# Clamp and shift of the float64 weight decode as scalar_tensor_tensor with a constant in PSUM, in place of tensor_scalar

## The chip, the cores and the metric

The kernel runs on one core of one Trainium2 chip. The metric is the device time of one execution in microseconds (us).

## What is computed

A two-dimensional Fourier transform (real part), then two dense networks over its 6016 tokens of 256 features. All weights arrive as float64, and the kernel turns them into float32 on the chip.

```python
X = np.fft.fft(np.fft.fft(x, axis=1), axis=2).real      # x: (2, 3008, 256)
x = X.reshape(6016, 256)
gate = 1.0 / (1.0 + np.exp(-(x @ w_gate)))              # first network, d_ff 1536
x = gate * (x @ w_val) @ moe_w_out
h = x @ w_in                                            # second network, d_ff 2048
out = (h * np.cos(h)) @ moe2_w_out
```

## The kernel before, in words

Three stages follow one another: the transform (stages a, b and c, to about 83 us of the profile), the first network (to about 518 us) and the second network (to the end). The transform leaves the tokens in `eo[t]`, six tiles of 2 x 1004 columns, each an even and an odd half. Every float32 operand of a matmul is split into a high and a low part, so that one product takes three matmuls (`three`, L493 to L495).

The first network runs 72 **steps**, `step1(s)`, s = 12 t + f, for six token tiles t and twelve blocks f of 128 hidden features. TensorE (PE) does 24 matmuls of 128x502 in a step:

- `ab(s, 0)` (6 matmuls) into PSUM banks 4 and 5, then `ab(s, 1)` (6 matmuls) into banks 6 and 7. The last three of `ab(s, 1)` write bank 7.
- `out1(s - 4)` (12 matmuls, L533, L535, L536) into banks 0 to 3; the four L533 stand at its end.

VectorE (DVE) then serves `even(s)`, two L511 that read banks 4 and 5, and `tokens(s)`, two L519 that read banks 6 and 7. These four banks have no second copy: `ab(s + 1, 0)` waits for the L511 of step s, `ab(s + 1, 1)` for its L519. ScalarE (ACT) takes the sigmoid (L667), GpSimd (POOL) multiplies gate and value (two L523, `times`), ACT makes the high part (L607, L608), and a DMA from POOL's queue (L546) adds the low part.

Beside this, 35 **units** of weights are decoded, each 128x512 float64 (the first smaller). A unit is a list of steps in `dec_steps` and `unit_steps`: a load (SP's queue, L148), two activations on ACT (L123, L124), then on VectorE the clamp (L127), the left shift by three (L129) and the sign (L131), on POOL an integer add (L134), and the split into high and low part (L139 on ACT, L140 mostly on POOL). Units of the second network are written to DRAM (`ws`, L167) and loaded again into `wr` late in the first network (L551). The tokens of the next tile are split into `es` in the same way (L139, L140) at the steps 5 and 6 of the first tile and around the steps 17, 29, 41, 53 and 64.

What runs between the fixed instructions is set by a planner at build time: `fill(e, until)` puts a unit's next step on engine e as long as its estimated cost (the number in the step's tuple, plus `beside[0]` = 0.5 us for VectorE in the first network) ends before `until`. So a change of a cost moves instructions, on VectorE and, through the times when units become ready, on the other engines' queues.

The clamp and the shift before are

```python
(V, .34, lambda: V.tensor_scalar(out=every(t), in0=every(t), scalar1=FMIN, scalar2=FMAX,
                                 op0=ALU.max, op1=ALU.min)),
(V, .34, lambda: V.tensor_scalar(out=every(u), in0=every(u), scalar1=3, scalar2=0x7FFFFFFF,
                                 op0=ALU.logical_shift_left, op1=ALU.bitwise_and)),
```

where t is the unit's 128x512 float32 buffer in SBUF, u the same bytes as uint32, and `every` a view of 2 x 256.

Of the kernel before, what the change touches and what calls it, by code (L numbers as in the profile page):

```python
# [12 lines left out]
U32 = mybir.dt.uint32  # L13
AF = mybir.ActivationFunctionType
ALU = mybir.AluOpType
# [29 lines left out]
FMIN = float(np.uint32(0x38000000).view(np.float32)) * 2.0 ** -80  # L45
FMAX = float(np.uint32(0x47EFFFFF).view(np.float32)) * 2.0 ** -80
# [3 lines left out]
def fft_moe_moe(ctx: ExitStack, tc: tile.TileContext, x, x0, head, w1, w1s, wo1, w2, t1, t3, out):  # L50
# [10 lines left out]
    V, A, G, PE = nc.vector, nc.scalar, nc.gpsimd, nc.tensor  # L61
# [8 lines left out]
    ps = pp.tile([128, 8, 512], F32, name="ps")  # L70
# [33 lines left out]
    VG = (V, G)  # L104

    def spend(e, us, after=0.0):
        clk[e] = max(clk[e], after) + us
        return clk[e]

    def dec_steps(buf, n):  # L110

        r = buf[:, 0:2 * n].rearrange("p (n t) -> p n t", t=2)
        lo, hi = r[:, :, 0], r[:, :, 1]
        t = buf[:, 2 * n:3 * n]
        u = t.bitcast(U32)

        def every(a):

            return a.rearrange("p (n k) -> p k n", k=2)

        return [

            (A, .52, lambda: A.activation(out=t, in_=hi, func=AF.Abs, scale=2.0 ** -80)),  # L123
            (A, .52, lambda: A.activation(out=lo.bitcast(I32), in_=lo.bitcast(U32), func=AF.Copy,  # L124
                                          scale=2.0 ** -29)),

            (V, .34, lambda: V.tensor_scalar(out=every(t), in0=every(t), scalar1=FMIN, scalar2=FMAX,  # L127
                                             op0=ALU.max, op1=ALU.min)),
            (V, .34, lambda: V.tensor_scalar(out=every(u), in0=every(u), scalar1=3, scalar2=0x7FFFFFFF,  # L129
                                             op0=ALU.logical_shift_left, op1=ALU.bitwise_and)),  # L130
            (V, .6, lambda: V.scalar_tensor_tensor(out=u, in0=hi.bitcast(U32), scalar=0x80000000, in1=u,  # L131
                                                   op0=ALU.bitwise_and, op1=ALU.bitwise_or)),

            (G, 1.23, lambda: G.tensor_tensor(out=t.bitcast(I32), in0=t.bitcast(I32), in1=lo.bitcast(I32),  # L134
                                              op=ALU.add)),
        ]
# [7 lines left out]
    def unit_steps(kind, i, buf):  # L144
        n = 2 * NF1 if kind == "row" else UC
        src = {"row": w1s, "w1": w1[i % NF1], "wo1": wo1[i % 6], "w2": w2[i]}[kind]
        t = buf[:, 2 * n:3 * n]
        steps = [(DQ, 1.5 * n / UC, lambda: DQ.dma_start(out=buf[:, 0:2 * n].bitcast(U32), in_=src.bitcast(U32)))]  # L148
        steps += dec_steps(buf, n)
        if kind == "row":  # L150
            steps.append((A, .2, lambda: A.copy(w128, t)))
        elif kind == "w1":

            d, m = t[:, 0:256], t[:, 256:512]
            steps += [(VG, .34, lambda e: e.tensor_tensor(out=buf[:, 0:256], in0=d, in1=m, op=ALU.add)),
                      (VG, .34, lambda e: e.tensor_tensor(out=buf[:, 256:512], in0=d, in1=m, op=ALU.subtract))]
            steps += hilo_steps(W1[:, i, :, :, 0], W1[:, i, :, :, 1],
                                buf[:, 0:512].rearrange("p (e g m) -> p g e m", e=2, g=2))
        elif kind == "wo1":
            steps += hilo_steps(WO1[:, 2 * i:2 * i + 2, 0], WO1[:, 2 * i:2 * i + 2, 1],  # L160
                                t.rearrange("p (f m) -> p f m", f=2))
        else:

            q = 4 if i < 8 else 2
            dst = buf[:, 0:2 * UC].bitcast(F32R).rearrange("p (q h m) -> p q h m", q=q, h=2)
            steps += hilo_steps(dst[:, :, 0], dst[:, :, 1], t.rearrange("p (q m) -> p q m", q=q))
            steps.append((DQ, 1.5, lambda: DQ.dma_start(out=ws[i], in_=buf[:, 0:2 * UC])))  # L167
        return steps
# [8 lines left out]
    beside = [0.0]  # L177

    def cost(step, e):
        return step[1] * (2.05 if step[0] is VG and e is G else 1) + (beside[0] if e is V else 0)  # L180

    def step_of(un, e=None):
        step = un[2].pop(0)
        if step[0] is VG:
            e = e or min(VG, key=lambda q: clk[q])
            step[2](e)
        else:
            e = step[0]
            step[2]()
        un[3] = spend(e, cost(step, e), un[3]) + (2.3 if e is DQ else .15)  # L190
        if not un[2]:
            live.remove(un)
            if un[1]:
                free.append([un[1][0], un[1][1], un[3]])
# [6 lines left out]
    def fill(e, until):  # L201

        while True:
            for un in live:
                step = un[2][0]
                if step[0] is VG and e is G and max(un[3], clk[V]) + VADV < max(un[3], clk[G]):
                    continue
                if e in step[0] if step[0] is VG else e is step[0]:
                    if max(un[3], clk[e]) + cost(step, e) <= until:
                        step_of(un, e)  # L210
                        break
            else:
                if e is DQ and len(todo) > held[0] and clk[e] + 1.5 <= until:
                    for bf in free:
                        if bf[2] <= until and max(clk[e], bf[2]) + LIFE <= bf[1]:
                            start(bf)
                            break
                    else:
                        return
                    continue  # L220
                return
# [483 lines left out]
    gate_at = 0.0  # L705
    LIFE, VADV = 0.0, 100.0
    beside[0] = .5
    free[:] = [bf for bf in free if bf[1] == ALWAYS]
    step1(0)
    now = stage_c(1, 1, AHC)  # L710
# [111 lines left out]
```

## Time and profile before

| | |
|---|---|
| runs shown | 1037.24, 1037.32, 1041.18 us; median 1037.32 us |
| profiled execution: span, first to last instruction | 1037.8 us |
| PE busy | 1004.8 us, 97% |
| VectorE busy | 779.9 us, 75% |
| ScalarE busy | 766.1 us, 74% |
| POOL busy | 668.7 us, 64% |

The profiled execution is known by its span alone, and that is 0.5 us above the median of the runs; nothing is added around it. Matmuls are pipelined, so a matmul shows 390 ns while a new one starts every 227 ns; the distance of two starts is the measure. PEclk is the granted TensorE clock as a share of 2.4 GHz.

### The profile page before, as it was taken

How to read it: one execution, taken by the hardware profiler on the slowest of the kernel's cores; microseconds unless marked ns; L12 is line 12 of the kernel's file. 1: busy time of each engine (PE TensorE's matmuls, PEld its weight loads, DVE VectorE, ACT ScalarE, POOL GpSimd, SP SyncE). 2: the span in 40 equal slices, each digit the busy share in tenths (PEclk: the TensorE clock that was granted, in tenths of full speed). 3: DMA queues.
4: the chain of work that ended last, by engine and by line, in shares of the span. 5: the costliest groups of instructions: out<-in, count | busy, mean ns of one | idle time of the engine just before them, and what ended most of it. 6: DMA issues, size and time to landing. Idle time of an engine off the chain costs nothing.

```text
span 1037.8 us, 13153 instructions
## 1 busy us (share of the span) xinstructions
PE 1004.8 (97%) x4566; PEld 835.8 (81%) x4566; DVE 779.9 (75%) x1029; ACT 766.1 (74%) x1208; POOL 668.7 (64%) x521
## 2 busy tenths in 40 slices
PE   8888899999898999999999999999999999999998
PEld 8877688788786888888788888888888888888886
DVE  5698887877778777776577777777777777777775
ACT  4765466567555667675698888988889888888886
POOL 3686687777666778776364656657466565665753
PEclk9998999999998999999999999999999999999999
DMA  9711457566664666688600000000000000000000
GB/s 293 234 68 53 88 128 173 123 139 136 154 144 106 140 150 150 140 229 218 176 1 20 1 21 0 21 21 1 20 1 21 20 1 21 0 20 21 1 20 21
DMA packets 25363, 85.59 MB, mean 82 GB/s; under 512 B 3248, under 2 KB 6640, under 8 KB 24624
## 3 DMA queue, kind: packets, MB, share of 16 engines
q0 software_dynamic: 10368, 37.02, 19.0%
q1 hardware_dynamic: 14672, 47.59, 13.6%
q8 instruction: 36, 0.59, 0.2%
q14 instruction: 31, 0.25, 0.1%
q10 hardware_dynamic: 256, 0.14, 0.1%
HBM read 33.16 MB, written 14.56 MB: 46 GB/s over the span
## 4 chain that ended last, share of the span: by engine, by line
PE 83%; DVE 9%; DMA 2%; ACT 2%; issue 2%; POOL 1%; SPq 0%; DVEq 0%; ACTq 0%; POOLq 0%
PE ps L575 25%; PE ps L493 14%; PE ps L494 14%; PE ps L495 13%; PE ps L533 5%; PE ps L535 5%; PE ps L536 5%; DVE D L519 4%; DVE D L127 2%; PE ps L437 1%; DMA gh<-D 1%; DVE D L129 1%; DMA eo<-in_w_dram 1%; ACT gh L607 1%; DVE D L511 1%
## 5 line engine op out<-in xcount | busy, mean ns | idle before, releaser
L601 POOL TENSOR_TENSOR h<-D,h 128x502 fp32r<-128x502 f32 x191 | 285.4, 1494 | 214.9 <-ACT h L600 203.1
L575 PE MATMUL ps<-h,wr 128*128 128x502 f32 x1152 | 291.8, 389 | 0.0
L493 PE MATMUL ps<-es,wr 128*128 128x502 f32 x672 | 265.5, 395 | 16.4 <-DVE D L519 10.0
L494 PE MATMUL ps<-es,wr 128*128 128x502 f32 x672 | 264.2, 393 | 0.0
L495 PE MATMUL ps<-es,wr 128*128 128x502 f32 x672 | 263.3, 392 | 0.0
L575 PEld LDWEIGHTS ps<-h,wr 128*128 128x128 f32 x1152 | 217.4, 189 | 44.7
L523 POOL TENSOR_TENSOR D<-D 128x502 f32<-128x502 f32 x144 | 185.1, 1335 | 101.0 <-ACT D L667 99.4
L586 DVE SCALAR_TENSOR_TENSOR D<-D,ps 128x502 f32<-128x502 int32 x192 | 130.2, 678 | 117.9 <-POOL h L601 109.1
L519 DVE TENSOR_TENSOR D<-D,ps 128x1004 f32<-128x1004 f32 x144 | 172.9, 1201 | 54.0 <-PE ps L495 30.3
L667 ACT ACTIVATE D<-D 128x1004 f32<-128x1004 f32 x72 | 75.2, 1044 | 157.3 <-DVE D L519 157.3
L493 PEld LDWEIGHTS ps<-es,wr 128*128 128x128 f32 x672 | 127.4, 190 | 47.7 <-DVE D L519 13.2
L587 DVE SCALAR_TENSOR_TENSOR D<-D 128x502 f32<-128x502 int32 x192 | 144.9, 755 | 6.6
L495 PEld LDWEIGHTS ps<-es,wr 128*128 128x128 f32 x672 | 127.8, 190 | 26.9
L494 PEld LDWEIGHTS ps<-es,wr 128*128 128x128 f32 x672 | 127.9, 190 | 25.5
L585 ACT ACTIVATE D<-ps 128x502 int32<-128x502 f32 x192 | 113.2, 590 | 46.8 <-PE ps L495 44.7
L593 DVE TENSOR_TENSOR D<-D,ps 128x502 f32<-128x502 f32 x192 | 128.9, 671 | 16.1 <-ACT D L592 16.1
L591 ACT ACTIVATE D<-D 128x502 f32<-128x502 f32 x192 | 119.2, 621 | 12.7 <-DVE D L587 10.4
L511 DVE SCALAR_TENSOR_TENSOR D<-eo,w,ps 128x502 f32<-128x502 f32 x144 | 101.8, 736 | 32.2 <-PE ps L495 31.8
L592 ACT ACTIVATE D<-D 128x502 f32<-128x502 f32 x192 | 120.0, 625 | 6.1
L600 ACT CAST h<-D 128x502 fp32r<-128x502 f32 x192 | 114.6, 597 | 0.2 <-DVE D L593 0.2
L535 PE MATMUL ps<-gh,wr 128*128 128x502 f32 x288 | 113.7, 395 | 0.0
L536 PE MATMUL ps<-gh,wr 128*128 128x502 f32 x288 | 112.6, 391 | 0.0
(86 smaller groups left out, 1071.1 us busy)
## 6 DMA issues: line engine op xcount, KB each, us to landing
gh<-D POOLq DMA_DIRECT2D x72, 502.0 KB, 4.8
D<-in_w_dram SPq DMA_DIRECT2D x17, 512.0 KB, 5.1
ws<-D SPq DMA_DIRECT2D x16, 512.0 KB, 3.6
wr<-ws SPq DMA_DIRECT2D x16, 512.0 KB, 4.1
out_dram<-D SPq DMA_DIRECT2D x24, 251.0 KB, 3.4
eo<-in_w_dram SPq DMA_DIRECT2D x11, 512.0 KB, 6.8
raw<-in_x_dram SPq DMA_DIRECT2D x15, 256.0 KB, 5.9
D<-in_wo_dram SPq DMA_DIRECT2D x5, 512.0 KB, 4.5
```

The costliest lines, as they stand in the source:

```text
L493: PE.matmul(o, w_hi, m_hi, start=first, stop=False)
L494: PE.matmul(o, w_lo, m_hi, start=False, stop=False)
L495: PE.matmul(o, w_hi, m_lo, start=False, stop=last)
L519: V.tensor_tensor(out=gv[s][:, :, c:c + PC], in0=sas, in1=ps[:, 6:8, 0:PC], op=op)
L523: G.tensor_tensor(out=gv[p][:, 1, m], in0=gv[p][:, 1, m], in1=gv[p][:, 0, m], op=ALU.mult)
L535: PE.matmul(o, WO1[:, f, 0, m], h[:, 0, sl], start=(f == 0), stop=False)
L536: PE.matmul(o, WO1[:, f, 1, m], h[:, 0, sl], start=False, stop=False)
L575: PE.matmul(o, WO2[:, f, i, d * 128:(d + 1) * 128], h[:, m], start=(f == 0 and i == m == 0), stop=(f == NF2 - 1 and m == 1))
L586: V.scalar_tensor_tensor(out=r, in0=k, scalar=-C1, in1=h, op0=ALU.mult, op1=ALU.add)
L587: V.scalar_tensor_tensor(out=r, in0=k, scalar=-C2, in1=r, op0=ALU.mult, op1=ALU.add)
L593: V.tensor_tensor(out=r, in0=r, in1=ps[:, 4 + s % 4, 0:PC], op=ALU.mult)
L601: (V if s == N2S - 1 else G).tensor_tensor(out=h[:, 1], in0=r, in1=f32(h[:, 0]), op=ALU.subtract)
```

## The change

From just before step 0 of the first network on (`spare[0] = True`), the clamp and the shift of a unit are `scalar_tensor_tensor` instructions over 128x512: the first constant is the immediate scalar, the second is a PSUM column that is broadcast along the row. The two columns are 510 and 511 of bank 7, which the matmuls of the networks (502 columns) leave alone; two memsets of 128x1 fill them. The planner's cost of either goes from 0.34 to 0.6 us. Units whose clamp and shift lie before that point keep `tensor_scalar`.

```diff
+    spare = [False]
+    cmax, cmask = ps[:, 7, 510:511], ps[:, 7, 511:512].bitcast(U32)
+
+    def two():
+        return .6 if spare[0] else .34
+
+    def clamp(t, te):
+        if spare[0]:
+            V.scalar_tensor_tensor(out=t, in0=t, scalar=FMIN, in1=cmax.to_broadcast(list(t.shape)),
+                                   op0=ALU.max, op1=ALU.min)
+        else:
+            V.tensor_scalar(out=te, in0=te, scalar1=FMIN, scalar2=FMAX, op0=ALU.max, op1=ALU.min)
+
+    def shift(u, ue):
+        if spare[0]:
+            V.scalar_tensor_tensor(out=u, in0=u, scalar=3, in1=cmask.to_broadcast(list(u.shape)),
+                                   op0=ALU.logical_shift_left, op1=ALU.bitwise_and)
+        else:
...
-            (V, .34, lambda: V.tensor_scalar(out=every(t), in0=every(t), scalar1=FMIN, scalar2=FMAX,
-                                             op0=ALU.max, op1=ALU.min)),
-            (V, .34, lambda: V.tensor_scalar(out=every(u), in0=every(u), scalar1=3, scalar2=0x7FFFFFFF,
-                                             op0=ALU.logical_shift_left, op1=ALU.bitwise_and)),
+            (V, two, lambda: clamp(t, every(t))),
+            (V, two, lambda: shift(u, every(u))),
...
     def cost(step, e):
-        return step[1] * (2.05 if step[0] is VG and e is G else 1) + (beside[0] if e is V else 0)
+        us = step[1]() if callable(step[1]) else step[1]
+        return us * (2.05 if step[0] is VG and e is G else 1) + (beside[0] if e is V else 0)
...
     beside[0] = .5
+    V.memset(cmax, FMAX)
+    V.memset(cmask, 0x7FFFFFFF)
+    spare[0] = True
```

The change adds 20 lines ahead of most of the code: L118 and L125 are the new clamp and shift, L150 is the old L131, L531 the old L511, L539 the old L519, L513 to L515 the old L493 to L495.

**VectorE, steps 29 to 31 of the first network, before** (D is the tile that holds the units' buffers and the gate and value buffers, ps the PSUM tile; L511 and L519 stand for one step each):

```order
L511 SCALAR_TENSOR_TENSOR D_73<-eo_67,w_71,ps 128x502 x2
L519 TENSOR_TENSOR D_73<-D_73,ps 128x2x502 x2
L127 TENSOR_SCALAR D_73<-D_73 128x2x256
L129 TENSOR_SCALAR D_73<-D_73 128x2x256
L511 SCALAR_TENSOR_TENSOR D_73<-eo_67,w_71,ps 128x502 x2
L519 TENSOR_TENSOR D_73<-D_73,ps 128x2x502 x2
L131 SCALAR_TENSOR_TENSOR D_73<-D_73 128x512
L511 SCALAR_TENSOR_TENSOR D_73<-eo_67,w_71,ps 128x502 x2
```

and the same place now:

```order
L531 SCALAR_TENSOR_TENSOR D_73<-eo_67,w_71,ps 128x502 x2
L539 TENSOR_TENSOR D_73<-D_73,ps 128x2x502 x2
L118 SCALAR_TENSOR_TENSOR D_73<-D_73,ps 128x512
L531 SCALAR_TENSOR_TENSOR D_73<-eo_67,w_71,ps 128x502 x2
L539 TENSOR_TENSOR D_73<-D_73,ps 128x2x502 x2
L125 SCALAR_TENSOR_TENSOR D_73<-D_73,ps 128x512
L531 SCALAR_TENSOR_TENSOR D_73<-eo_67,w_71,ps 128x502 x2
```

Before, clamp and shift stood side by side in one step and the sign in the next; now each of the three has a step of its own, at most one a step. It is so for all 18 units that are decoded in the first network, between the steps 5 and 65.

**PE, `ab(30, 1)`, before** (es is the split token tile, wr the weights; the first three write bank 6, the last three bank 7; the waits are those that stand on the instruction):

```order
L493 MATMUL ps<-es_92,wr 128x502 [waits DVE_49]
L494 MATMUL ps<-es_92,wr 128x502
L495 MATMUL ps<-es_92,wr 128x502
L493 MATMUL ps<-es_92,wr 128x502
L494 MATMUL ps<-es_92,wr 128x502
```

and now:

```order
L513 MATMUL ps<-es_92,wr 128x502 [waits DVE_49]
L514 MATMUL ps<-es_92,wr 128x502
L515 MATMUL ps<-es_92,wr 128x502
L513 MATMUL ps<-es_92,wr 128x502 [waits DVE_49]
L514 MATMUL ps<-es_92,wr 128x502
```

The matmul that opens bank 7 has a wait on VectorE of its own in the steps that hold a clamp or a shift, since these read bank 7. The order of PE's instructions is unchanged.

## Rows read from the trace of the kernel before

**Rows 1.** The page, part 1: busy time, share of the span and instructions

```profile
PE 1004.8 (97%) x4566; PEld 835.8 (81%) x4566; DVE 779.9 (75%) x1029; ACT 766.1 (74%) x1208; POOL 668.7 (64%) x521
```

**Rows 2.** Windows: length, busy us (instructions) of PE, PEld, DVE, ACT, POOL; PEclk, DMA

```profile
250.00:275.00 25.00, 21.97 (x89) 17.49 (x89) 19.93 (x19) 14.30 (x18) 19.49 (x17) 0.93 0.58 125
```

**Rows 3.** Timeline of PE: start, length, line; idle time before and its releaser

```profile
116.07 1.07 PE L533 MATMUL ps<-gh,wr 128*128 128x502 f32 x4
...
127.16 1.07 PE L533 MATMUL ps<-gh,wr 128*128 128x502 f32 x4
...
198.24 1.09 PE L533 MATMUL ps<-gh,wr 128*128 128x502 f32 x4
...
205.63 1.08 PE L533 MATMUL ps<-gh,wr 128*128 128x502 f32 x4
...
254.82 1.07 PE L533 MATMUL ps<-gh,wr 128*128 128x502 f32 x4
...
257.77 0.39 PE L493 MATMUL ps<-es,wr 128*128 128x502 f32 x1
...
260.28 1.06 PE L533 MATMUL ps<-gh,wr 128*128 128x502 f32 x4
262.72 0.50 PE L493 MATMUL ps<-es,wr 128*128 128x502 f32 x1 [1.37 <-DVE D L511]
...
266.00 0.79 PE L493 MATMUL ps<-es,wr 128*128 128x502 f32 x1 [1.66 <-DVE D L519]
...
270.74 1.08 PE L533 MATMUL ps<-gh,wr 128*128 128x502 f32 x4
...
325.43 1.07 PE L533 MATMUL ps<-gh,wr 128*128 128x502 f32 x4
...
338.20 1.06 PE L533 MATMUL ps<-gh,wr 128*128 128x502 f32 x4
```

**Rows 4.** Timeline of DVE, same columns

```profile
6.53 0.06 DVE L316 MEMSET halfpi<- 128x1 f32 x1
...
111.40 6.43 DVE L127 TENSOR_SCALAR D<-D 128x512 f32<-128x512 f32 x1
...
193.67 4.19 DVE L127 TENSOR_SCALAR D<-D 128x512 f32<-128x512 f32 x1
...
251.15 1.43 DVE L511 SCALAR_TENSOR_TENSOR D<-eo,w,ps 128x502 f32<-128x502 f32 x2 [0.91 <-PE ps L495]
253.36 2.44 DVE L519 TENSOR_TENSOR D<-D,ps 128x1004 f32<-128x1004 f32 x2 [0.78 <-ACT gh L608]
256.64 5.38 DVE L129 TENSOR_SCALAR D<-D 128x512 uint32<-128x512 uint32 x1
...
321.70 5.46 DVE L127 TENSOR_SCALAR D<-D 128x512 f32<-128x512 f32 x1 [0.77 <-ACT D L123]
```

**Rows 5.** Timeline of POOL, same columns

```profile
253.18 2.81 POOL L523 TENSOR_TENSOR D<-D 128x502 f32<-128x502 f32 x2
255.64 1.18 POOL L546 DMA_DIRECT2D gh<-D  x1
256.25 1.69 POOL L140 TENSOR_TENSOR es<-eo,es 128x502 fp32r<-128x502 f32 x1
257.51 1.68 POOL L140 TENSOR_TENSOR D<-D 128x512 fp32r<-128x512 f32 x1
258.76 2.87 POOL L523 TENSOR_TENSOR D<-D 128x502 f32<-128x502 f32 x2
```

**Rows 6.** One line's instructions: duration ns min/median/max, first and last start

```profile
L129 DVE TENSOR_SCALAR D<-D x22: 428/430/5380, 68.6 to 448.8; 128x512 uint32<-128x512 uint32 x22
L131 DVE SCALAR_TENSOR_TENSOR D<-D x22: 682/684/1652, 70.4 to 453.8; 128x512 uint32<-128x512 uint32 x22
L519 DVE TENSOR_TENSOR D<-D,ps x144: 1199/1201/1203, 87.6 to 496.5; 128x1004 f32<-128x1004 f32 x144
L586 DVE SCALAR_TENSOR_TENSOR D<-D,ps x192: 677/678/681, 500.0 to 1026.1; 128x502 f32<-128x502 int32 x192
```

More of the change, by code (lines that the diff above doesn't have):

```diff
@@ L108, in spend @@
         return clk[e]
+    spare = [False]
[13 more added lines that the diff above has]
+        else:
+            V.tensor_scalar(out=ue, in0=ue, scalar1=3, scalar2=0x7FFFFFFF,
+                            op0=ALU.logical_shift_left, op1=ALU.bitwise_and)
     def dec_steps(buf, n):
```

## The prediction

> **What bounds the kernel now.** I read the page first: PE is busy for 97% of the span [rows 1], so only time in which PE waits or runs slowly can be gained. The windows of 25 us show where that is. In the first network a few of them hold too little work: the one from 250 us has 89 matmuls at a granted clock of 0.93 [rows 2], where 25 us at the pace of an undisturbed step (24 matmuls in 5.46 us, below) are 110. PE's timeline shows why: in an undisturbed step the last matmuls of a step (L533) follow those of the step before by 260.28 - 254.82 = 5.46 us, but the next ones come only at 270.74, and between them PE waits twice, for a L511 and for a L519 of VectorE [rows 3].
>
> VectorE's timeline names what it was doing: the shift of a weight unit that begins at 256.64 takes 5.38 us [rows 4], where its median is 0.43 [rows 6]. It waits for no semaphore; it runs long. POOL's timeline explains it: from 256.25 to 261.63 POOL has four tensor_tensor back to back, each started before the one ahead of it has ended, and the shift ends at 262.02, just behind the last [rows 5]. The clamps at 111.40 (6.43 us), 193.67 (4.19) and 321.70 (5.46) are the same [rows 4]; PE's matching distances are 11.09, 7.39 and 12.77 us in place of 5.46 [rows 3]. So one kind of VectorE instruction cannot get in beside a run of POOL instructions, and four times that starves PE through its single-buffered PSUM banks.
>
> **What does not suffer.** The two L519 that run from 253.36 to 255.80 lie wholly inside a run of POOL work [rows 4, 5], and all 144 L519 take between 1199 and 1203 ns. The 192 L586, a scalar_tensor_tensor with one operand in SBUF and one in PSUM, take 677 to 681 ns [rows 6], while POOL is busy for 64% of the span [rows 1]. The new clamp and shift are of that form.
>
> **The change part by part.**
>
> *Removed: the four stalls.* PE's loss in each is the distance of its L533 less 5.46 us [rows 3]:
> - 127.16 - 116.07 = 11.09: 5.63
> - 205.63 - 198.24 = 7.39: 1.93
> - 270.74 - 260.28 = 10.46: 5.00
> - 338.20 - 325.43 = 12.77: 7.31
>
> Together 19.87 us. This holds the waits and the matmuls after them at a lower clock (the 0.93 of that window [rows 2]). I count the whole: the new instructions lie at other steps, but the reason for a stall is gone wherever they lie.
>
> *Added: longer instructions.* 18 units, 36 instructions, go from 0.43 us (L129's median) to 0.69. That price is L586's 678 ns for 502 columns, some 10 ns more for 512; the two-SBUF form L131 has a median of 684 [rows 6]. It is 36 x 0.26 = 9.4 us of VectorE time. On the path: in the new order a step holds one of them. VectorE idles 0.91 us ahead of L511 and 0.78 ahead of L519 in a step without unit work [rows 4]; 0.69 fits into the first gap. I take 0. The Trainium skill speaks against the change here: "VectorE: DVE Perf Modes", section "Why PSUM operands drop a tier", says that any PSUM operand takes an fp32 instruction down to one element per cycle, where a tensor_scalar from SBUF to SBUF can do two. The rows agree in size (0.43 against 0.69), and by that rule alone the change could only cost.
>
> *Added: a wait of PE.* The matmul that opens bank 7 in `ab(s, 1)` now waits for the clamp or shift of its step. That instruction starts when L519 ends, at 255.80 in step 30 [rows 4], and would end at 256.49; bank 7 is opened at 257.77, as the tenth matmul of the step [rows 3]. So the slack is 1.28 us. Price 0. Behind this matmul the whole of PE's queue would wait, and a clamp over 1.28 us late would show at once.
>
> *Added: two memsets* of 128x1, 0.06 us each by L316 [rows 4], before step 0 in a busy stretch of VectorE: 0.1 us, taken in full.
>
> *Moved.* Since each unit takes three steps of VectorE and not two, the units' integer adds and splits on POOL, their activations on ACT and a few loads on SP's queue move by a step or two; the last unit is done one step later (its sign in step 65, was 64), well before the end of the first network, and SP has one load less behind it. PE's order is the same. I price this at 0 to 1 us, for a wait of a step's fraction at a tile boundary, and take 0. POOL is next in line: with two extra tensor_tensor, which start 1.26 us apart, and 256.25 - 255.64 = 0.61 us for the DMA issue [rows 5] a step of POOL is 4 x 1.26 + 0.61 = 5.65 us against PE's 5.46. That is a delay of 0.2 us in such a step, and its product is wanted by `out1` four steps later: covered.
>
> **Sum.** 1037.8 (the span of the profiled execution) - 19.87 + 0.1 = 1018.0. The median of the runs is 0.5 us lower: 1017.5 us.
>
> **The rivals.**
>
> *A. The stall moves to the sign (L131), 1022 to 1025 us.* It reads two SBUF operands and keeps its form. It has been held up before: 1652 ns against a median of 684 [rows 6]. In the new order it meets POOL's split of a token tile at the steps 29, 54 and 65. If each costs what the shortest stall cost (1.93 us), the time is 1017.5 + 5.8 = 1023.3. Against it: its longest delay is 0.97 us, less than one POOL instruction, and it starts right at the end of L519, before POOL's next extra. Chance 0.12. The Trainium skill bears on this: "SBUF — State Buffer", in the part that reads its diagram of the ports, says that VectorE instructions in a two-port mode or with two SBUF inputs share a locked port pair with GpSimd, and that the loser is blocked for the whole instruction. The trace agrees that somebody is blocked; but 5.38 us is four POOL instructions, not one, which the page does not tell.
>
> *B. The new form starves as well, 1052 us, slower.* Reading a constant from PSUM would then not free the instruction of POOL, and clamp and shift, now in two steps, meet twice as many runs of POOL: the steps 5, 6, 17, 18, 30, 41 and 42 have a token split, most with a second POOL instruction beside it. At the mean of the four stalls (19.87 / 4 = 4.97) that is 7 x 4.97 = 34.8, or 1017.5 + 34.8 = 1052.3. It is slower than before from the fifth stall on. Against it stand the 336 instructions with one PSUM operand of which none took over 4 ns more than the shortest of its line [rows 6]; a broadcast column is the one thing that none of these has. Chance 0.03.
>
> *C. The longer instructions are on the path, 1027 us.* If VectorE had no gap, all 9.4 us would count: 1017.5 + 9.4 = 1026.9. The idle 0.91 us [rows 4] is against it. Chance 0.03. Of the 9.4 us the Trainium skill's rule on PSUM operands gives the cause.
>
> *D. The time was lost anyway, 1032 to 1038 us.* At the stalls the split of the next tile runs on POOL and ACT; PE could wait for that in place of VectorE. Against it: the split tile is wanted some six steps later, and no wait of PE in [rows 3] is for POOL. Chance 0.04. That the change does not do what it says is excluded by the order: 36 instructions have the new form.
>
> **How the numbers follow.** Forecast 0.78 (1016.5 to 1019.5: the stalls' sum is read from starts, and another reference step, 5.45 to 5.48, moves it by 0.1; the rest is the 0 to 1 us for moved work, and as much on the other side for small delays that go with the stalls), A 0.12, C 0.03, D 0.04, B 0.03. The range 1015.8 to 1024.0 holds the forecast and most of A. Faster by over 0.5%, about what a measurement of this kernel can tell from no change, is below 1032.1: forecast, A, C and a little of D, 0.94. I give 0.93, same 0.04, slower 0.03.
>
> **What would show it right or wrong.** Right: the new clamp and shift take 0.68 to 0.75 us, shortest and longest alike, also inside runs of POOL; no window between 125 and 480 us has fewer than 110 matmuls or a clock below 0.98; PE has no idle time for L511 or L519 after step 4; the second network takes the same time, so the span shrinks by 19 to 20 us, all of it ahead of 340 us. Wrong: a new instruction of over 2 us (B); a sign of over 2 us with PE waiting behind it (A); PE idle for the clamp or shift at bank 7; POOL or a DMA as the releaser of PE's waits at a tile boundary (D).

## The result, and the profile after

The changed kernel takes 1025.45 us (median of 4 runs, 1025.05 to 1027.88); the kernel before, on the same chip, 1039.25 us (4 runs, 1037.24 to 1041.52). The ratio is 0.9878, 95% interval 0.9855 to 0.9902: faster by 1.2%, where 1017.5 us (1.9%) were predicted, and outside the range, above its 1024.0. The span of the profiled execution went from 1037.8 to 1023.3 us; its time is 1025.05 us, so 1.75 us lie outside the span.

The page, part 1, of the changed kernel, against [rows 1]:

```profile
PE 997.5 (97%) x4566; PEld 831.1 (81%) x4566; DVE 774.7 (76%) x1031; ACT 766.3 (75%) x1208; POOL 668.5 (65%) x521
```

PE is busy for 7.3 us less, though it does the same matmuls; its mean granted clock went from 0.988 to 0.993, so fewer of them run at the low clock. The instructions of the clamp, the shift and the sign (duration ns min/median/max, first and last start), against [rows 6]:

```profile
L118 DVE SCALAR_TENSOR_TENSOR D<-D,ps x18: 678/680/689, 110.2 to 431.4; 128x512 f32<-128x512 f32 x18
L125 DVE SCALAR_TENSOR_TENSOR D<-D,ps x18: 678/680/680, 115.7 to 436.8; 128x512 uint32<-128x512 uint32 x18
L150 DVE SCALAR_TENSOR_TENSOR D<-D x22: 682/686/5415, 70.2 to 442.3; 128x512 uint32<-128x512 uint32 x22
```

The new clamp and shift are as priced: no instance is over 689 ns. The third line is the miss: the sign, which the change does not touch, now takes up to 5415 ns, where its longest was 1652 [rows 6]. VectorE's timeline shows where, at the steps 29 and 65, with step 54 between them:

```profile
241.36 5.42 DVE L150 SCALAR_TENSOR_TENSOR D<-D 128x512 uint32<-128x512 uint32 x1
...
382.14 1.68 DVE L150 SCALAR_TENSOR_TENSOR D<-D 128x512 uint32<-128x512 uint32 x1
...
442.27 4.88 DVE L150 SCALAR_TENSOR_TENSOR D<-D 128x512 uint32<-128x512 uint32 x1
```

POOL's timeline at the first and at the second of these:

```profile
241.19 0.88 POOL L566 DMA_DIRECT2D gh<-D  x1 [1.60 <-issue]
241.80 1.59 POOL L159 TENSOR_TENSOR es<-eo,es 128x502 fp32r<-128x502 f32 x1
243.04 2.83 POOL L543 TENSOR_TENSOR D<-D 128x502 f32<-128x502 f32 x2
245.50 1.21 POOL L566 DMA_DIRECT2D gh<-D  x1
246.11 1.71 POOL L159 TENSOR_TENSOR es<-eo,es 128x502 fp32r<-128x502 f32 x1
...
381.57 1.69 POOL L159 TENSOR_TENSOR es<-eo,es 128x502 fp32r<-128x502 f32 x1
383.38 2.81 POOL L543 TENSOR_TENSOR D<-D 128x502 f32<-128x502 f32 x2
```

At step 29 the split (L159) and the two products (L543) follow one another without a break from 241.80 to 243.04 + 2.83 = 245.87. The sign ends at 246.78, 0.91 us after the run: one undisturbed sign of 0.68 and little more. At step 54 the split ends at 381.57 + 1.69 = 383.26 and the products start only at 383.38; the sign ends at 383.82, so it went in at that break. In these two places a sign takes 1.68 us where the split and the products leave a break, and 5.42 us where they close up; E10 tests this.

PE behind the two long signs, against [rows 3]:

```profile
246.02 1.06 PE L553 MATMUL ps<-gh,wr 128*128 128x502 f32 x4
247.47 0.50 PE L513 MATMUL ps<-es,wr 128*128 128x502 f32 x1 [0.39 <-DVE D L531]
...
250.79 0.79 PE L513 MATMUL ps<-es,wr 128*128 128x502 f32 x1 [1.69 <-DVE D L539]
...
255.61 1.06 PE L553 MATMUL ps<-gh,wr 128*128 128x502 f32 x4
...
446.94 1.08 PE L553 MATMUL ps<-gh,wr 128*128 128x502 f32 x4
451.16 0.50 PE L513 MATMUL ps<-es,wr 128*128 128x502 f32 x1 [1.68 <-DVE D L539]
454.46 1.07 PE L553 MATMUL ps<-gh,wr 128*128 128x502 f32 x4
```

The distances are 9.59 and 7.52 us in place of 5.46, so the signs cost 4.13 + 2.06 = 6.19 us. After the first one the next matmuls run at a lower clock, which the window shows (100 matmuls at 0.93; undisturbed ones hold 111 or 112 at 1.00); behind the second one the window from 450 us shows 1.00, and 1.68 of its 2.06 us are the one wait of PE:

```profile
250.00:275.00 25.00, 24.21 (x100) 20.04 (x101) 19.54 (x23) 15.82 (x19) 18.17 (x16) 0.93 0.58 125
```

**A ruler that leaves the start out.** Runs of one kernel differ by several us, and the spans below differ by up to 7 us ahead of step 0 alone. So kernels are compared from the first matmul of `out1(0)` in step 4 to the end of the span; all the stalls lie behind it. Before: 1037.8 - 108.79 = 929.01 us; after: 1023.3 - 107.54 = 915.76 us. That is 13.25 us less, and 19.87 (the four old stalls) less 6.19 (the signs) is 13.68. The other 1.25 us of the two spans' difference lie in the start. Such a rest is that of one execution: E3's is the fastest of its ten runs, E9's the slowest of its five. The matmuls in question (timeline of PE, before and after):

```profile
108.79 0.39 PE L535 MATMUL ps<-gh,wr 128*128 128x502 f32 x1
```

```profile
107.54 0.39 PE L555 MATMUL ps<-gh,wr 128*128 128x502 f32 x1
```

### The profile page after: what moved, and what is told of

Its sections match the earlier page's. It is cut to its first block, busy times and chain, and to the rows that moved or that the text cites. A ratio compares the mean times of both kernels' runs of the same rounds, so it can differ in the third digit from the quotient of the medians.

```text
span 1023.3 us, 13172 instructions
## 1 busy us (share of the span) xinstructions
PE 997.5 (97%) x4566; PEld 831.1 (81%) x4566; DVE 774.7 (76%) x1031; ACT 766.3 (75%) x1208; POOL 668.5 (65%) x521
## 4 chain that ended last, share of the span: by engine, by line
PE 88%; DVE 5%; DMA 3%; issue 2%; ACT 1%; SPq 0%; ACTq 0%; POOL 0%; DVEq 0%; POOLq 0%
PE ps L595 26%; PE ps L513 15%; PE ps L514 14%; PE ps L515 14%; PE ps L553 6%; PE ps L555 6%; PE ps L556 6%; DVE D L539 2%; DMA raw<-in_x_dram 1%; PE ps L457 1%; DMA gh<-D 1%; PE ps L363 1%; DVE D2l L443 1%; DMA xs<-in_x_dram 1%; DMA eo<-in_w_dram 1%
## 5 line engine op out<-in xcount | busy, mean ns | idle before, releaser
L513 PE MATMUL ps<-es,wr 128*128 128x502 f32 x672 | 263.6, 392 | 8.3 <-DVE D L539 7.4
L515 PE MATMUL ps<-es,wr 128*128 128x502 f32 x672 | 261.7, 389 | 0.0
L543 POOL TENSOR_TENSOR D<-D 128x502 f32<-128x502 f32 x144 | 184.6, 1324 | 86.1 <-ACT D L687 83.4
L539 DVE TENSOR_TENSOR D<-D,ps 128x1004 f32<-128x1004 f32 x144 | 172.9, 1201 | 53.6 <-PE ps L515 33.4
L513 PEld LDWEIGHTS ps<-es,wr 128*128 128x128 f32 x672 | 126.7, 188 | 37.9 <-DVE D L539 9.5
L515 PEld LDWEIGHTS ps<-es,wr 128*128 128x128 f32 x672 | 126.8, 189 | 26.5
L531 DVE SCALAR_TENSOR_TENSOR D<-eo,w,ps 128x502 f32<-128x502 f32 x144 | 101.9, 736 | 23.3 <-PE ps L515 23.0
```

What stands on the lines that cost most here:

```text
L513: PE.matmul(o, w_hi, m_hi, start=first, stop=False)
L515: PE.matmul(o, w_hi, m_lo, start=False, stop=last)
L539: V.tensor_tensor(out=gv[s][:, :, c:c + PC], in0=sas, in1=ps[:, 6:8, 0:PC], op=op)
L543: G.tensor_tensor(out=gv[p][:, 1, m], in0=gv[p][:, 1, m], in1=gv[p][:, 0, m], op=ALU.mult)
```

## The experiments

The theory: an instruction of VectorE whose tensor operands all lie in SBUF is held up by a run of POOL's tensor_tensor until the run breaks, whatever instruction it is; with one operand in PSUM it is not. What the change left behind is the sign, which is of the first kind. The remaining time behind the first matmul of `out1(0)` ("rest") is in this table, with the medians; "before" was 1039.63, 1038.99 and 1040.21 us beside the three groups (E1 to E4, E5 to E8, E9 to E11).

| kernel | median us | ratio to before, 95% | profiled span | rest | stalls behind step 4 |
|---|---|---|---|---|---|
| before | see above | | 1037.8 | 929.0 | 3 clamps, 1 shift |
| after | 1025.45 | 0.9855 to 0.9902 | 1023.3 | 915.8 | 2 signs |
| E1 order only | 1040.56 | 0.9996 to 1.0035 | 1038.8 | 930.4 | 3 clamps, 1 shift, 2 signs |
| E2 form only | 1021.92 | 0.9817 to 0.9866 | 1018.4 | 911.4 | 1 sign |
| E3 constants in SBUF | 1040.77 | 0.9983 to 1.0024 | 1032.5 | 926.5 | 3 clamps, 1 shift, 1 sign |
| E4 sign early | 1021.00 | 0.9799 to 0.9858 | 1016.5 | 909.2 | none |
| E5 clamp only | 1035.16 | 0.9936 to 0.9970 | 1033.4 | 923.9 | 4 shifts |
| E6 memsets on POOL | 1026.90 | 0.9861 to 0.9897 | 1026.0 | 916.4 | 2 signs |
| E7 constants at the start | 1020.23 | 0.9797 to 0.9832 | 1019.8 | 911.8 | none |
| E8 after, again | 1028.17 | 0.9864 to 0.9907 | 1028.5 | 915.3 | 2 signs |
| E9 constants before stage b | 1017.48 | 0.9764 to 0.9796 | 1019.9 | 909.3 | none |
| E10 split late | 1019.86 | 0.9786 to 0.9817 | 1018.6 | 909.3 | none |
| E11 sign early, again | 1020.91 | 0.9800 to 0.9834 | 1018.7 | 909.0 | none |

### E1 and E2: the order alone, the form alone

E1 keeps the change's costs, and so its order, with the old instructions:

```diff
     def clamp(t, te):
-        if spare[0]:
+        if False:
...
     def shift(u, ue):
-        if spare[0]:
+        if False:
```

> The order of the change (planner's cost 0.6) with the old tensor_scalar for clamp and shift. Theory F (the form decides: any VectorE instruction that takes two SBUF reads at a time is held up by an unbroken run of POOL instructions): clamp and shift now meet the token splits at the steps 5, 6, 17, 18, 30, 41, 42, so at least three of them take over 3 us, and the time is that of before or more, 1034 to 1050 us. Rival O (the new order brought the gain, one instruction a step instead of two): no clamp or shift over 2 us, 1019 to 1027 us.

Measured: 1040.56 us, no gain. As many stalls of the clamp and the shift are there as before, and two signs have come on top. The clamp and the shift of E1, by line:

```profile
L121 DVE TENSOR_SCALAR D<-D x22: 417/764/6409, 68.4 to 447.0; 128x512 f32<-128x512 f32 x22
L128 DVE TENSOR_SCALAR D<-D x22: 421/736/4458, 69.4 to 452.4; 128x512 uint32<-128x512 uint32 x22
```

E2 has the new instructions at the old costs, and so the order of before:

```diff
     def two():
-        return .6 if spare[0] else .34
+        return .34
```

> The new form in the order of before (planner's cost 0.34, so clamp and shift side by side again and the sign in the step behind). Theory F: clamp and shift take 0.68 us everywhere, the signs stand where none was held up for over 1.1 us before, so all four stalls of before are gone and none comes: 19.9 us less than before, about 1019 to 1020 us, 6 us less than the change. Rival L (two instructions of 0.68 us in one step are too long for PE's slack of 1.28 us at bank 7): PE idle in the 18 steps with such a pair, 1024 to 1032 us. Rival O: as before, 1037 to 1041 us.

Measured: 1021.92 us and a rest of 911.4, 4.3 us less than with the change (915.8). So the form brings the gain and the order gives some of it back. One sign is still held up, at step 42, where before none was, for 4.52 us:

```profile
312.57 4.52 DVE L150 SCALAR_TENSOR_TENSOR D<-D 128x512 uint32<-128x512 uint32 x1
```

In the order of before the sign stands there too. What moved is its time: before, the clamp of step 41 had been held up 5.46 us [rows 4], and the sign came behind all that, at 332.60, while POOL waited 5.38 us for a sigmoid of ScalarE; it took 0.69 us. With this stall gone the sign meets the split that starts on POOL at 312.39 and the two products behind it. So a stall hid a later one. The two rows of before, VectorE and POOL:

```profile
332.60 0.69 DVE L131 SCALAR_TENSOR_TENSOR D<-D 128x512 uint32<-128x512 uint32 x1
...
333.84 2.49 POOL L523 TENSOR_TENSOR D<-D 128x502 f32<-128x502 f32 x2 [5.38 <-ACT D L667]
```

### E3: is it the form, or the operand in PSUM?

```diff
-    halfpi = cpool.tile([128, 1], F32, name="halfpi")
+    hp3 = cpool.tile([128, 3], F32, name="halfpi")
+    halfpi = hp3[:, 0:1]
...
-    cmax, cmask = ps[:, 7, 510:511], ps[:, 7, 511:512].bitcast(U32)
+    cmax, cmask = hp3[:, 1:2], hp3[:, 2:3].bitcast(U32)
```

> The change with its two constants in SBUF columns in place of PSUM; same order, same form of instruction. Theory F (two SBUF operands are what is held up, as in the sign): clamp and shift are held up at the steps with a token split, maxima of 3 us and more, time 1030 to 1050 us. Rival R (only the tensor_scalar at two elements per cycle is held up; the sign's two long ones have another reason): clamp and shift 0.68 us everywhere, 1024 to 1027 us as with the change.

Measured: 1040.77 us, no gain. The same instructions, with their constant column in SBUF:

```profile
L119 DVE SCALAR_TENSOR_TENSOR D<-D,halfpi x18: 684/1002/6648, 108.6 to 442.9; 128x512 f32<-128x512 f32 x18
L126 DVE SCALAR_TENSOR_TENSOR D<-D,halfpi x18: 682/832/4481, 119.1 to 448.3; 128x512 uint32<-128x512 uint32 x18
```

The shortest is as long as with PSUM (684 against 678), but the longest is 6648 ns and not 689. So what helps is that the second operand is in PSUM, and not that tensor_scalar is gone.

### E4, E11 and E10: the sign away from the split, and the split away from the sign

E4 lets VectorE's planner run 1.1 us further in the steps 28 and 64, so that the sign stands one step earlier (at each place one instruction on POOL and one on ScalarE move with it); E11 is the same kernel in another group:

```diff
-            ahead(V, now + 3 * MM)
+            ahead(V, now + 3 * MM + (1.1 if s in (28, 64) else 0))
```

> The change with the signs of the steps 29 and 65 pulled one step ahead, behind the shift of the steps 28 and 64, by more time for the planner there. Theory F: the two signs of 5.42 and 4.88 us are gone, PE's 4.13 and 2.06 us with them, 1019 to 1020 us. Rival D (PE's loss at these tile boundaries comes from POOL and ScalarE being late there, whatever VectorE does): 1025 us as with the change, with PE waiting for something else at the steps 29 and 65.

> The changed kernel with the sign of the steps 29 and 65 one step ahead, once more, on the same chip as the two others. No clamp, shift or sign over 1.7 us after step 4; 909 to 912 us from the first matmul of `out1(0)` to the end of the span; time 1018 to 1024 us, of which the start of the program (when the input has landed) makes most of the spread.

Measured: 1021.00 and 1020.91 us, a rest of 909.2 and 909.0 us, and a sign of at most 1680 ns. E10 leaves VectorE as it is and moves the other side, the piece of the split on POOL:

```diff
+    wait_split = [False]
...
+                if step[0] is VG and wait_split[0] and un[0][0] in ("es", "ys"):
+                    continue
                 if step[0] is VG and e is G and max(un[3], clk[V]) + VADV < max(un[3], clk[G]):
...
         main = s < N1S
+        wait_split[0] = s in (29, 65)
```

> The changed kernel, in which the piece of the token split that POOL runs in the steps 29 and 65 comes one step later (behind the shift's and the integer add's step); VectorE's order is that of the change, and its sign stays in the steps 29 and 65. Theory P (the sign is held up by the split's tensor_tensor, which starts behind the DMA issue and joins with the two products to one run): without it POOL idles there until the sigmoid is done, so both signs take 0.68 to 1.7 us; span 1016 to 1019 us after correction for the start of the step 0, time 1018 to 1022 us, 6 us below the change on the same chip. Rival S (the two steps hold VectorE up for another reason, for instance ScalarE's copies of the split): signs of 4.9 to 5.4 us remain, and the time is that of the change.

Measured: 1019.86 us and a rest of 909.3. VectorE and POOL at step 29 in E10:

```profile
243.14 0.68 DVE L150 SCALAR_TENSOR_TENSOR D<-D 128x512 uint32<-128x512 uint32 x1
```

```profile
242.99 0.88 POOL L569 DMA_DIRECT2D gh<-D  x1 [1.60 <-issue]
244.40 2.52 POOL L546 TENSOR_TENSOR D<-D 128x502 f32<-128x502 f32 x2 [0.53 <-ACT D L691]
```

Same sign, same step, same place behind the DMA issue: 0.68 us without the split, 5.42 with it. It also shows that POOL's DMA issue (242.99 to 243.87) does not hold the sign up. On ScalarE one activation of the split moves along at step 29 and nothing at step 65, where the sign takes 0.68 us too, so rival S did not happen. That the same sign is short without the split, and short when it is moved, settles what the 6.19 us were: the rest is 915.3 and 915.8 us in the two traces of the change, and 909.0 to 909.3 in these three, 6.0 to 6.8 us less.

### E5: half of the cure

E5 has the new clamp and the old shift, in the order of before:

```diff
     def two():
-        return .6 if spare[0] else .34
+        return .34
...
     def shift(u, ue):
-        if spare[0]:
+        if False:
```

> Only the clamp has the new form; the shift is the old tensor_scalar and the planner's costs (so the order of the work) are those of before. Theory H (whatever instruction with its operands in SBUF alone stands first beside a run of POOL work is held up): the clamps take 0.68 to 0.69 us everywhere, and the stalls pass to the shifts behind them in the steps 5, 19, 30 and 41, each of 3.5 to 6 us; the time is 1033 to 1040 us. Rival C (each instruction is held up by itself, so half of the cure gives its share: three of the four long instructions of before were clamps): one or two stalls are left, 1023 to 1028 us.

```profile
L118 DVE SCALAR_TENSOR_TENSOR D<-D,ps x18: 679/680/686, 112.1 to 443.8; 128x512 f32<-128x512 f32 x18
L128 DVE TENSOR_SCALAR D<-D x22: 428/432/5698, 70.4 to 444.5; 128x512 uint32<-128x512 uint32 x22
```

Measured: 1035.16 us. Four shifts are held up, 5.70, 3.49, 5.50 and 4.73 us at the steps 5, 19, 30 and 41. Three of four long instructions of before were clamps, and curing the clamp brings 0.5% of the 1.6% that E2 brings with both: the first open instruction in the row inherits the wait.

### E6: a break in POOL's run

```diff
         m = slice(c, c + PC)
+        G.memset(hp3[:, 1:2], 0.0)
         G.tensor_tensor(out=gv[p][:, 1, m], in0=gv[p][:, 1, m], in1=gv[p][:, 0, m], op=ALU.mult)
```

(`hp3` is `halfpi` with a second column.)

> The changed kernel, with a memset of one SBUF column (128x1) on POOL ahead of each of its 144 products of gate and value (L543), so that POOL's tensor_tensor no longer follow one another without a break. Theory U (the sign is held up because POOL's tensor_tensor overlap, each started before the one ahead has ended; a break lets VectorE in): no sign takes over 2.7 us, PE has no wait over 0.5 us for VectorE at the steps 29 and 65, and the time is 6 us below that of the change, 1018 to 1021 us. Rival B (VectorE gets in only when POOL's queue has nothing to do, or the memset leaves no break): signs of 4.9 to 5.5 us stay at the steps 29 and 65, and the time is 1024 to 1027 us.

Measured: 1026.90 us; the signs take 6.84 and 4.71 us. POOL at step 29:

```profile
243.63 1.59 POOL L160 TENSOR_TENSOR es<-eo,es 128x502 fp32r<-128x502 f32 x1
244.84 0.41 POOL L544 MEMSET halfpi<- 128x1 f32 x1
244.90 1.59 POOL L545 TENSOR_TENSOR D<-D 128x502 f32<-128x502 f32 x1
246.10 0.42 POOL L544 MEMSET halfpi<- 128x1 f32 x1
246.16 1.59 POOL L545 TENSOR_TENSOR D<-D 128x502 f32<-128x502 f32 x1
247.36 1.22 POOL L568 DMA_DIRECT2D gh<-D  x1
247.97 1.73 POOL L160 TENSOR_TENSOR es<-eo,es 128x502 fp32r<-128x502 f32 x1
```

The rival holds: the signs stay long. By these rows the memset is no break. It starts at 244.84, before the split has ended at 243.63 + 1.59 = 245.22, and the product starts 0.06 us behind it. The sign started at 243.42 and ended only at 250.26, behind the second split: it did not use the 0.22 us between 246.16 + 1.59 = 247.75 and 247.97, where the change's sign went in at a break of 0.24 (245.87 to 246.11) and that of step 54 at 0.12.

The kernel before has such a case too, in the longest of its stalls, the clamp at 111.40 [rows 4]:

```profile
112.81 2.78 POOL L523 TENSOR_TENSOR D<-D 128x502 f32<-128x502 f32 x2
115.26 1.17 POOL L546 DMA_DIRECT2D gh<-D  x1
115.86 1.68 POOL L140 TENSOR_TENSOR es<-eo,es 128x502 fp32r<-128x502 f32 x1
```

The products end at 112.81 + 2.78 = 115.59 and the next split starts 0.27 us later, but the clamp ends at 117.83, behind that split. The first stalls of E1, E3 and E5 reach over breaks of 0.28 to 0.29 us in the same way. So this clamp, which the prediction calls the same as the others, waited for more than an unbroken run, and the length of a break does not tell whether VectorE gets in. POOL's spans are rough; what ends a wait stays open.

### E7, E9 and E8: the same form in the transform; the base once more

E7 sets the constants at the very start, so that the 17 units of the transform have the new form too; E9 sets them between the stages a and b. Both have E4's line. In E9 the planner's cost of a clamp or shift stays 0.34 up to step 0. The edit of E9, without that line:

```diff
     def two():
-        return .6 if spare[0] else .34
+        return .6 if beside[0] else .34
...
-    nbank = [0, 8]
+    spare[0] = True
+    V.memset(cmax, FMAX)
+    V.memset(cmask, 0x7FFFFFFF)
+    nbank = [0, 7]
...
     beside[0] = .5
-    V.memset(cmax, FMAX)
-    V.memset(cmask, 0x7FFFFFFF)
-    spare[0] = True
```

> The changed kernel with the sign of the steps 29 and 65 moved a step ahead (as in the run before that did so), and the two constants set at the very start, so that all 35 units use the new form; stage b of the transform then leaves out bank 7. Theory H: the 17 clamps and 17 shifts of the transform, 0.74 to 0.77 us on average now with the longest near 1.5 us, take 0.68 to 0.69 us; PE's waits for VectorE in the transform (1.45 us at 77 us, 2.06 at 54 us) get shorter by 0 to 3 us in all: 1018 to 1021 us. Rival N (VectorE is not what those waits hang on, and one bank less in stage b costs some): 1021 to 1024 us.

> The changed kernel with the sign of the steps 29 and 65 one step ahead, and the two constants set between stage a and stage b of the transform, so that the clamps and shifts of stages b and c have the new form too; stage b leaves out bank 7. With the constants set at the very start the time from the first matmul of stage b to step 0 was 38.2 us, against 42.6 to 42.8 us elsewhere, but stage a's first matmuls waited until 6.88 us. Theory H: here the 38 to 40 us come without that wait, and the time is 1015 to 1019 us. Rival N (the shorter stages b and c were only the other side of the later start: ScalarE and VectorE had been given time to work ahead): 42 to 43 us from stage b to step 0, and 1019 to 1023 us.

> The changed kernel once more, on the same chip as the three others, as the base for them. 1023 to 1028 us; signs of 4.9 to 5.5 us at the steps 29 and 65, no clamp or shift of the new form over 0.70 us. If the two long signs lay at other steps, or if there were none, then what holds them up would hang on the moment and not on the order.

E8 confirms the base: signs of 5.42 and 4.88 us at the same steps and a rest of 915.3 us. E7 took 1020.23 us, inside its forecast, but with other parts: stages b and c take 38.2 us, 4.6 less than in E4, but the start loses as much. PE's timeline of E7:

```profile
6.88 2.48 PE L348 MATMUL ps<-warm 128*128 128x128 f32 x10 [6.88 <-DVE ps L338]
...
26.84 11.85 PE L365 MATMUL ps<-hd,raw 128*128 128x96 f32 x104 [2.35 <-DVE eo L125]
...
486.88 2.04 PE L555 MATMUL ps<-gh,wr 128*128 128x502 f32 x4 [2.40 <-DMA gh<-D]
```

The first matmuls wait for a memset of the constants until 6.88 us (1.00 before); in stage a one waits 2.35 us for a shift that reads bank 7. The third row is why E7's rest is 911.8 without a stall: the wait for a DMA is 2.40 us there, against 0.87 to 1.25 in the others, and in the 5 us from 485 us the granted clock is 0.66, where E4's is 1.00. In E9 the two waits of the start are gone, stages b and c take 84.89 - 44.87 = 40.0 us (42.5 in E11), and 1017.48 us is the best of all; its interval lies wholly below E11's, of the same group. Its fastest and slowest runs (1016.11 and 1021.75) still overlap with E11's (1019.50 to 1023.05). The times and the 40.0 us fit theory H. In E9's trace stage b begins 2.9 us later than in E11's (44.87 against 42.01), so step 0 comes no earlier there (84.89 against 84.54). That is rival N's case, but a late stage b alone does not shorten what follows: in E8 it begins at 45.90 and the two stages take 42.75 us. Which of the waits in stages b and c went was not taken apart.

## Why the prediction was wrong

**What held.** PE was bound by the four stalls, and their sum was right: without them, and without the signs, the rest is 909.0 to 909.3 us (E4, E9, E10, E11; E7 has 911.8 with its longer wait for a DMA), and 929.01 - 19.87 is 909.14. The new instructions take 0.68 us everywhere, as priced from the 678 ns of L586 [rows 6]. They cost nothing on the path, and in the changed kernel PE never waits for them at bank 7 behind step 4 (in E2, which has both in one step, once for 0.08 us). The Trainium skill's rule that a PSUM operand takes the faster mode away ("VectorE: DVE Perf Modes", "Why PSUM operands drop a tier") would have missed the sign of the result: each instruction is 0.25 us longer (680 ns against 430), and the kernel is 1.2% faster. No run shows this rule by itself. In E3 the same instruction with its constant in SBUF takes no less, 682 to 684 ns at the shortest, so the 0.25 us come with the form of two tensor operands wherever the second one lies, and rival C's sentence that the rule gives the cause is not borne out.

**The step that failed** is in *Removed*: "I count the whole: the new instructions lie at other steps, but the reason for a stall is gone wherever they lie." The reason, a run of POOL that shuts out VectorE's instructions with operands in SBUF alone, was gone for the clamp and the shift and not for the sign, which the same change moves. Rival A said so, named the steps 29, 54 and 65 and priced them at 5.8 us; 29 and 65 happened, for 6.19 us. It was given 0.12, for two wrong reasons. "Its longest delay is 0.97 us, less than one POOL instruction" was no evidence: it fits a run of one POOL instruction, as at step 54 now, and only shows that no sign of before had met a closed run; the one at step 42 had been spared by the stall ahead of it (E2). "It starts right at the end of L519, before POOL's next extra" is true (241.36 against 241.80) and does not help: the sign had started first, and it lost all the same. The likelier reading was that the sign is as open as the clamp, since both have SBUF operands alone; E3, where the two-operand form is held up 6.65 us, shows it directly. The prediction's own sum for A, 1023.3, shows the digits of the measured span by chance: it is a time, to be set against 1025.45, and it counts three signs at 1.93 us where two cost 4.13 and 2.06.

**The second miss is the base**: "The median of the runs is 0.5 us lower." The sum was made in the span, and nothing was added around it; but in all twelve profiled executions whose time is on record (all but that of before) the time is 1.7 to 1.9 us more than the span (1025.05 against 1023.3). So the span of 1037.8 belonged to a run of some 1039.6 us, 2.3 above the median of the three runs shown, and a forecast span of 1018.0 is a time of about 1019.8. In E10, where the forecast's premise holds, it came to 1019.86 us. Neither miss alone leads out of the range: 1017.5 + 6.19 is 1023.7, below its 1024.0.

**In sum**: 1017.5 + 6.19 (the signs) + 2.3 (span and base) - 1.25 (the start of this execution) = 1024.7 us, against 1025.05 of the profiled execution. Some 0.3 us stay unexplained; the one other wait of PE, 0.87 us for a DMA at 491 us, is no part of it, since the kernel before has it too (1.08 us at 506). Rivals B, C and D did not happen: no new instruction over 0.69 us, no wait for them, and with the stalls gone the whole 19.87 us come back.

## What to carry to other kernels

When a cure is for one kind of operand, list every instruction of this kind near the conflict, those the change leaves alone included; the one left over inherits the wait (E5, and the sign here). In these kernels a run of POOL's tensor_tensor shuts out VectorE's tensor_scalar and two-operand scalar_tensor_tensor that read SBUF alone, for 3.5 to 6.8 us, and an instruction of VectorE that PE waits for is best given a PSUM operand or a place where POOL idles. Compare two kernels from the first instruction behind the noise, not by span or median alone: here the rest came back within 0.2 us (E4 and E11) and 0.5 us (the change and E8) when a kernel was traced twice, while two medians of the changed kernel lay 2.7 us apart.

## What the runs showed of the hardware that was not expected

- The wait is as long as a row of POOL's tensor_tensor, 3.5 to 6.8 us here, not as one of them (1.2 to 1.3 us from start to start), and at times it reaches over a short break in the row (E6). The Trainium skill, "SBUF — State Buffer", in the part on its diagram of the ports, says that whichever starts first has the shared ports for the whole instruction. The sign of step 29 started 0.44 us before the split and did not end before the products had; on POOL, spans are rough, so the order of the starts is not certain to that.
- A constant column of PSUM, broadcast along a row of 512, costs nothing over one in SBUF (678 against 684 ns at the shortest), and 18 x 2 such instructions were never held up in any of the nine profiled kernels that have both (690 ns at most).
- Much of the spread between runs lies ahead of step 0: the first matmul of `ab(0, 0)` comes at 81.5 us in E3 and at 88.65 in E8, with the same transform. In E8, PE's stage a waits 2.40 us for input at 34.95 and the 64 matmuls that follow take 10.38 us, 162 ns each; in the other trace of the same kernel 104 of them take 11.81 us, 114 ns each.

```profile
34.95 10.38 PE L363 MATMUL ps<-hd,raw 128*128 128x96 f32 x64 [2.40 <-DMA raw<-in_x_dram]
```
